# Attention, four experts and a gated layer on one core: seven half-size products parted at token 640 instead of 768

## The chip, the cores and the metric

The program runs on one core of one Trainium2 chip. The metric is the device time of one execution in microseconds (us), lower is better. An execution is profiled besides; its trace gives every instruction's start and duration. PE is the matrix engine, PEld its weight loads, DVE the vector engine, ACT the scalar engine, POOL the GpSimd engine, SP the engine that issues the transfers.

## The reference, cut to what matters

```python
scores = q @ k.T / 8; keep the 32 largest of each row of 576; softmax; x = attn @ v   # 2 x 8 heads, head size 64
x = x.reshape(1152, 512)                                                           # tokens x model
p = probs / probs.sum(-1)
x = sum(p[:, e:e+1] * (relu(x @ w1[e]) @ w2[e]) for e in range(4))                 # hidden size 1024
out = ((x @ w_a) * (x @ w_b)) @ w_out                                              # hidden size 1536
```

## The kernel before

The 1152 tokens are nine tiles of 128, in four groups of 1, 2, 3 and 3 tiles (`GROUPS`): columns 0 to 127, 128 to 383, 384 to 767 and 768 to 1151 of the transposed activations `xs`, which are kept as a high and a low part (`xs[:, 0]`, `xs[:, 1]`). A product of two such operands is three matmuls: high by high, high by low, low by high. Attention of a group feeds the experts of that group (`experts`), whose result `y` is turned on PE (`tr`) and written back to `xs` (`replace`, for groups 2 and 3 `combine`). Then comes the gated layer (`gated`), for 6 blocks of two units of w_a, w_b (`d_unit`).

The pair of products x w_a and x w_b of a unit is made by seven products of half the size (`product`, `multiply`). The tokens are parted in two sets (`sets`), each set in two halves of tokens; the seven products take sums of the halves (S1 to S4, made in `combine`, stored in `xt`) with sums of the weights. One product is 2 x 3 matmuls whose width is one half: 384 columns in set 0 (tokens 0 to 767), 192 in set 1 (tokens 768 to 1151). There are 12 units, so 12 x 42 = 504 matmuls for each set. DVE adds the seven results into a buffer `tp` (line 1315), ACT makes the first copy (line 1324), POOL multiplies the gates (line 1318), ACT and POOL split the product into high and low (lines 1335 and 1336), and `second` multiplies it with w_out; its results are added by DVE (line 1360) and leave by SP. All matmuls have line 487, all turns line 490, since helpers record them.

Set 1's halves lie wholly in the last group; set 0's in groups 0 to 2. `combine` of the last group runs between the first two sets of products of the gated layer (`pending`).

Psum has eight banks of 512 columns. In the last stage six (`pps`) take the half-size products and two (`ns`) the results of `second`. Buffers are named pools (`Slots`); a pool gives its buffers out in a fixed order, and a buffer's next user waits for its last one.

Nothing is ordered by hand: every step is an `Op` with an estimated duration, a key and its waits, and `Plan.best` makes 42 trial orders with `Plan.order`, replays each with `Plan.rerun`, and emits the order with the least mean. Each engine then runs its list in order. A change of one estimated duration can so move instructions anywhere in the program.

Of the kernel before, what the change touches and what calls it, by code (L numbers as in the profile page):

```python
# [13 lines left out]
ALU = mybir.AluOpType  # L14
# [74 lines left out]
SEEN, SEEN_PE = 45, 130  # L89
ISSUE, LAND, GBS, LANES = 500, 2100, 320.0, 8  # L90
# [7 lines left out]
class Plan:  # L98
# [37 lines left out]
    def rerun(self, got, draw):  # L136

        free, end, dma, users = {}, {}, 0.0, {}
        last = 0.0
        for op in got:  # L140
            t = free.get(op.engine, 0.0)
            for w in op.waits:
                t = max(t, end[id(w)] + (SEEN_PE if op.engine == "PE" else SEEN))

            for b in op.tiles:
                u = users.get(id(b))
                if u is None:
                    u = users[id(b)] = [max([self.freed.get(k, 0.0) for k in b.slots.cells(b.slot)] or [0.0])]
                t = max(t, u[0] + (SEEN_PE if op.engine == "PE" else SEEN))
            if op.engine == "SP":  # L150
                free["SP"] = t + ISSUE
                dma = max(dma, t + ISSUE) + op.nbytes / GBS
                e = dma + LAND + draw.uniform(0.0, LATE_DMA)
            else:
                free[op.engine] = t + op.hold
                e = t + op.hold + op.lag + (draw.uniform(0.0, LATE_ENGINE) if op.engine != "PE" else 0.0)
            end[id(op)] = e
            last = max(last, e)
            for b in op.tiles:
                k = (b.slots.name, b.slot)  # L160
                self.freed[k] = max(self.freed.get(k, 0.0), e)
        self.freed.clear()
        return last

    def order(self):
# [57 lines left out]
        def pick(engine):  # L223
# [6 lines left out]
            while ready_:  # L230
                item = heapq.heappop(ready_)
                op = item[2]

                ok = not (op.port and free.get("POOL", 0.0) > now)
                for t in op.tiles:
                    if t.slot is None and (t.slots in stuck or place(t) is None):
                        stuck.add(t.slots)
                        ok = False
                if ok:
                    found = op  # L240
                    break
                skipped.append(item)
                if len(skipped) > 60:
                    break
# [4 lines left out]
        while len(done) < len(self.ops):  # L249
            moved = False  # L250
            for engine in free:
# [15 lines left out]
                if engine == "SP":  # L267
                    free[engine] = now + ISSUE
                    dma_free = max(dma_free, now + ISSUE) + op.nbytes / GBS
                    end = dma_free + LAND  # L270
                    lanes.append(end)
                else:
                    free[engine] = now + op.hold
                    end = now + op.hold + op.lag + op.late
# [41 lines left out]
def mm_r(n):  # L316
    return max(n, 96) / 2.4 + 13.3
# [18 lines left out]
def body(tc, q, k, v, probs, w1, w2, wa, wb, wo, out):  # L336
# [111 lines left out]
    tps = [low.slots("tpa", 1, 4 * 384), low.slots("tpb", 2, 4 * 192)]  # L448
# [182 lines left out]
    def start_pair(c, h2, n):  # L631
# [72 lines left out]
        for b in batches(tiles):  # L704
# [5 lines left out]
            if b not in vrem_done:  # L710
                vrem_done[b] = [
                    load(lambda b=b, j=j: vrem[b][j * REM:(j + 1) * REM, j::2], lambda b=b, j=j: last_rows(v, b)[:, j::2], n - 2.4, (), (), 65536, since=14e3)
# [251 lines left out]
    def second(hts, units, t0, after, bank=None, begin=True, end=True, last=None):  # L964
# [3 lines left out]
        for i, ((h, hd, n), (u, ud, uv, part)) in enumerate(zip(hts, units)):  # L968
# [7 lines left out]
            hd = hd[t0 // 384] if isinstance(hd[0], list) else hd  # L976
# [67 lines left out]
    sets = [(0, 384, 384), (768, 960, 192)]  # L1044
    xdone2, late_x = {}, []

    def combine(c, y, yd):
# [8 lines left out]
        xv = lambda i: xt.ap.rearrange("p (i o a n) -> p i o a n", i=2, o=3, a=2)[:, i, :, :, 384 * own:384 * own + n]  # L1056
        x0, x1 = slice(c0, c0 + n), slice(c1, c1 + n)
        K = -1500 if own else -1000
        got = []

# [9 lines left out]
        def pool(w, emit, key, after, tiles):  # L1070
            if own:
                return vector(dve(w), lambda: emit(nc.vector), key, after, tiles, port=True)
            return gpsimd(pool_(w), lambda: emit(nc.gpsimd), key, after, tiles)

        def half(a):
            tp = tps[own].tile()
            tv = lambda i, j=None: tp.ap[:, i * n:(j or i + 1) * n]
            (p, po), (q_, qo) = turned(a), turned(a + 2)
            if own:
                h1 = scalar(n, lambda: nc.scalar.activation(xs[:, 0, a, x0], p.ap[:, 0:n], AF.Copy), K, [po], [p])  # L1080
                l1 = vector(dve(n), lambda: nc.vector.tensor_tensor(xs[:, 1, a, x0], p.ap[:, 0:n], xs[:, 0, a, x0], op=ALU.subtract), K, [h1], [p])
                got.extend([h1, l1])
                f = [scalar(2 * n, lambda: nc.scalar.activation(tv(0, 2), p.ap[:, 0:2 * n], AF.Copy), K, [po], [p, tp])]
                qv = lambda: q_.ap[:, n:2 * n]
            else:
                f = [
                    pool(n, lambda e, k=k, i=i: e.tensor_tensor(tv(i), xs[:, 0, k, x0], xs[:, 1, k, x0], op=ALU.add), K, ydone[0, k] + ydone[1, k], [tp])
                    for k, i in ((a, 0), (a + 2, 2))
                ]
                f.append(scalar(n, lambda: nc.scalar.activation(tv(1), p.ap[:, 0:n], AF.Copy), K, [po], [p, tp]))  # L1090
                qv = lambda: q_.ap[:, 0:n]
            h = scalar(384, lambda: nc.scalar.activation(xs[:, 0, a + 2, cs], q_.ap[:, 0:384], AF.Copy), K, [qo], [q_])
            l = vector(dve(384), lambda: nc.vector.tensor_tensor(xs[:, 1, a + 2, cs], q_.ap[:, 0:384], xs[:, 0, a + 2, cs], op=ALU.subtract), K, [h], [q_])
            s1 = vector(dve(n), lambda: nc.vector.tensor_tensor(tv(3), qv(), tv(1), op=ALU.add), K, f + [qo], [q_, tp])
            s3 = pool(n, lambda e: e.tensor_tensor(tv(1), tv(1), tv(0), op=ALU.subtract), K, [s1], [tp])
            s2 = pool(n, lambda e: e.tensor_tensor(tv(0), tv(3), tv(0), op=ALU.subtract), K, [s3], [tp])
            if own:
                s4 = vector(dve(n), lambda: nc.vector.tensor_tensor(tv(2), q_.ap[:, 0:n], tv(0), op=ALU.subtract), K, [s2], [q_, tp])
            else:
                s4 = pool(n, lambda e: e.tensor_tensor(tv(2), tv(2), tv(0), op=ALU.subtract), K, [s2], [tp])  # L1100
            h1 = scalar(n, lambda: nc.scalar.activation(xs[:, 0, a, x1], tv(3), AF.Copy), K, [s1], [tp], sbuf=True)
            l1 = pool(n, lambda e: e.tensor_tensor(xs[:, 1, a, x1], tv(3), xs[:, 0, a, x1], op=ALU.subtract), K, [h1], [tp])
            t3 = lambda: tv(0, 3).rearrange("p (o n) -> p o n", o=3)
            h2 = scalar(3 * n, lambda: nc.scalar.activation(xv(0)[:, :, a], t3(), AF.Copy), K, [s4], [tp, xt], sbuf=True)
            l2 = pool(3 * n, lambda e: e.tensor_tensor(xv(1)[:, :, a], t3(), xv(0)[:, :, a], op=ALU.subtract), K, [h2], [tp, xt])
            got.extend([h, l, h1, l1, h2, l2])
        for a in range(2):
            half(a)
        xdone2[own] = got + ([] if own else sum((ydone[g, k] for g in range(2) for k in range(KD)), []))
# [163 lines left out]
    def gated():  # L1273
# [9 lines left out]
        def operand(i, own, hl, a):  # L1283
# [5 lines left out]
            return xt()[:, hl, i - 4, a, 384 * own:384 * own + w]  # L1289
# [16 lines left out]
        def multiply(un, own, g):  # L1306

            m = sets[own][2]
            tp = tps[own].tile()
# [30 lines left out]
        for f in range(F2 // 256):  # L1340
# [80 lines left out]
```

## Time and profile before

| what | value |
|---|---|
| time, median of 3 runs (range) | 847.09 us (846.9 to 849.94) |
| the profiled execution: time, span of its instructions | 847.36 us, 845.6 us |
| mean granted clock of PE | 0.988 |
| busy in the span: PE, PEld, DVE, ACT, POOL | 809.6, 720.0, 771.4, 537.3, 364.8 us |

The time is the whole execution's; the span runs from the first to the last instruction, 1.76 us less. Busy time of PE is from modelled ends, so two matmuls that overlap in the pipe are counted once; how dense they are is read from the distance between their starts.

### The profile page before, as it was taken

What the parts mean: (1) busy time and instruction counts of PE and PEld (TensorE: products, weight loads), DVE (VectorE), ACT (ScalarE), POOL (GpSimd) and SP (SyncE); (2) the same over time, 40 slices, a digit from 0 to 9 for tenths busy, and PEclk for the clock granted to TensorE, in tenths of its full rate; (3) what the DMA queues carried; (4) which work ended last, traced back from release to release, by engine and by line L of the source; (5) the groups of instructions that cost most, each with busy time, mean ns of one, the idle gap of its engine ahead of it and who ended that gap; (6) DMA issues with size and microseconds to landing.
All of it is one profiled execution on the core that took longest, in us unless ns stands there. A gap on an engine that the chain in (4) does not pass through costs nothing.

```text
span 845.6 us, 14637 instructions
## 1 busy us (share of the span) xinstructions
PE 809.6 (96%) x5285; PEld 720.0 (85%) x5285; DVE 771.4 (91%) x1507; ACT 537.3 (64%) x951; POOL 364.8 (43%) x335
## 2 busy tenths in 40 slices
PE   6589999999999999999999999999999999999997
PEld 5467777799888899998999988999889989999895
DVE  7989999999899999999976989998898988989973
ACT  6879887999888989987764656665444423323220
POOL 3524343788979668754210180000024426153431
PEclk9699999999999999999999999999999999999999
DMA  5939976755565343423344646887431312313013
GB/s 175 290 103 335 315 230 206 219 183 179 161 197 178 101 145 118 163 77 100 100 127 145 203 125 221 252 257 259 132 100 52 125 50 76 111 40 100 26 50 112
DMA packets 91416, 129.68 MB, mean 153 GB/s; under 512 B 10832, under 2 KB 67152, under 8 KB 89808
## 3 DMA queue, kind: packets, MB, share of 16 engines
q1 hardware_dynamic: 91344, 128.75, 48.0%
q8 instruction: 41, 0.67, 0.3%
q14 instruction: 31, 0.25, 0.1%
HBM read 115.36 MB, written 13.37 MB: 152 GB/s over the span
## 4 chain that ended last, share of the span: by engine, by line
PE 60%; DVE 22%; ACT 9%; POOL 5%; issue 3%; DMA 1%; POOLq 0%; DVEq 0%; ACTq 0%
PE ps L487 57%; DVE low L767 7%; DVE low L775 6%; PE ps L490 3%; ACT low L806 1%; POOL mid L933 1%; ACT low L817 1%; ACT mid L932 1%; ACT lowa L746 1%; DVE mid L933 1%; DVE big L1269 1%; ACT low L798 1%; DVE raw L1360 1%; ACT lowa L875 1%; POOL low L802 1%
## 5 line engine op out<-in xcount | busy, mean ns | idle before, releaser
L487 PE MATMUL ps<-mid 128*128 128x512 f32 x1092 | 282.2, 397 | 4.0 <-POOL mid L933 2.1
L487 PEld LDWEIGHTS ps<-mid 128*128 128x128 f32 x1092 | 199.3, 189 | 43.5 <-DVE raw L1360 4.0
L487 PE MATMUL ps<-xs,mid 128*128 128x384 f32 (+1 forms) x1152 | 206.1, 321 | 3.3 <-DVE mid L1006 2.6
L487 PEld LDWEIGHTS ps<-xs,mid 128*128 128x128 f32 x1152 | 185.2, 189 | 13.4 <-DVE mid L1006 4.2
L767 DVE MAX8 low<-low 128x8 f32<-128x576 f32 x216 | 154.8, 749 | 0.2
L1318 POOL TENSOR_TENSOR low<-low 128x384 f32<-128x384 f32 (+1 forms) x48 | 48.2, 1005 | 218.9 <-DVE low L1315 217.1
L933 POOL TENSOR_TENSOR mid<-raw,mid 128x1024 fp32r<-128x1024 f32 x48 | 115.0, 2404 | 9.5 <-ACT mid L932 7.3
L802 POOL TENSOR_TENSOR low<-lowa,low 128x576 f32<-128x576 f32 x70 | 101.3, 1462 | 31.1 <-ACT low L798 31.0
L932 ACT ACTIVATE mid<-raw 128x1024 fp32r<-128x1024 f32 x96 | 101.8, 1068 | 16.8 <-PE ps L487 8.5
L775 DVE MATCH_REPLACE8 low<-low 128x576 f32<-128x576 f32 x144 | 106.3, 745 | 0.0
L487 PE MATMUL ps<-xs,big 128*128 128x384 f32 (+1 forms) x576 | 93.3, 307 | 1.8 <-ACT low L1324 1.7
L487 PEld LDWEIGHTS ps<-xs,big 128*128 128x128 f32 x576 | 85.5, 190 | 4.9 <-ACT low L1324 2.0
L1315 DVE TENSOR_TENSOR low<-ps,low 128x384 f32<-128x384 f32 (+1 forms) x168 | 71.8, 449 | 17.0 <-PE ps L487 15.7
L1002 ACT ACTIVATE mid<-ps 128x384 fp32r<-128x384 f32 (+1 forms) x96 | 44.0, 460 | 45.1 <-PE ps L487 40.2
L487 PE MATMUL ps<-lowa_again,big 128*128 128x384 f32 (+1 forms) x432 | 70.8, 305 | 0.0
L933 DVE TENSOR_TENSOR mid<-raw,mid 128x1024 fp32r<-128x1024 f32 x48 | 62.5, 1305 | 5.9 <-ACT mid L932 5.8
L487 PEld LDWEIGHTS ps<-lowa_again,big 128*128 128x128 f32 x432 | 64.4, 190 | 1.4
L1006 DVE SCALAR_TENSOR_TENSOR mid<-ps,mid 128x384 fp32r<-128x384 f32 (+1 forms) x96 | 47.9, 503 | 16.9 <-ACT mid L1002 16.8
L798 ACT ACTIVATE low<-lowa,low 128x576 f32<-128x576 f32 x70 | 53.3, 782 | 12.7 <-POOL low L792 12.6
L817 ACT ACTIVATE low<-low 128x576 f32<-128x576 f32 x70 | 51.9, 782 | 12.3 <-DVE low L814 12.1
L490 PE MATMUL ps<-identr,low 128*128 128x128 f32 x360 | 51.9, 279 | 7.7 <-ACT low L817 7.7
L806 ACT ACTIVATE low<-low 128x576 f32<-128x576 f32 x70 | 54.8, 785 | 4.0 <-POOL low L802 4.0
(121 smaller groups left out, 1235.1 us busy)
## 6 DMA issues: line engine op xcount, KB each, us to landing
raw<-in_moe_w_dram SPq DMA_DIRECT2D x122, 512.0 KB, 3.8
big<-kscr SPq DMA_DIRECT2D x20, 576.0 KB, 5.6
low<-in_v_dram SPq DMA_DIRECT2D x24, 256.0 KB, 3.7
low<-in_moe_w_b_dram SPq DMA_DIRECT2D x12, 512.0 KB, 3.6
low<-in_moe_w_a_dram SPq DMA_DIRECT2D x12, 512.0 KB, 3.6
low<-in_moe_w_out_dram SPq DMA_DIRECT2D x12, 512.0 KB, 4.8
wscr<-big SPq DMA_DIRECT2D x6, 1024.0 KB, 5.5
mid<-wscr SPq DMA_DIRECT2D x6, 1024.0 KB, 4.7
```

Source lines behind the costliest of these rows:

```text
L487: nc.tensor.matmul(out, l, r, **kw)
L490: nc.tensor.transpose(out, a, i)
L767: 62 + 1.04 * width, lambda at=at, cs=cs: nc.vector.max(m8v()[:, x, cs], at()), key + 0.02 * r, [done],
L775: lambda at=at, cs=cs: nc.vector.match_replace(out=src[1](), in_to_replace=m8v()[:, x, cs], in_values=at(), imm_value=LOW),
L798: S, lambda x=x, s=s: nc.scalar.activation(ev(x), s.ap, AF.Relu, bias=endv()[:, x, 1:2], scale=-STEEP),
L802: pool_(S), lambda x=x, s=s: nc.gpsimd.tensor_tensor(ev(x), s.ap, ev(x), op=ALU.subtract), ks, [a], [s, ep]
L806: lambda x=x: nc.scalar.activation(ev(x), ev(x), AF.Exp, bias=endv()[:, x, 0:1], scale=scale, accum_out=sums.ap[:, x:x + 1]),
L817: S, lambda x=x: nc.scalar.activation(ev(x), ev(x), AF.Copy, scale=sums.ap[:, x:x + 1]),
L932: hi = scalar(1024, lambda: nc.scalar.activation(u.ap[:, 0:1024], r.ap, AF.Copy), 500 + s, [ld], [u, r], sbuf=True)
L933: sub = lambda eng: eng.tensor_tensor(u.ap[:, 1024:2048], r.ap, u.ap[:, 0:1024], op=ALU.subtract)
L1315: return vector(dve(m), lambda: nc.vector.tensor_tensor(tv(out), p.ap[:, 0:m], tv(i), op=ALU.add), K, [o] + after, [p, tp])
L1318: return gpsimd(pool_(m), lambda: nc.gpsimd.tensor_tensor(tv(out), tv(i), tv(j), op=ALU.mult), K, after, [tp])
```

## The change

The sets become tokens 0 to 639 in halves of 320, and tokens 640 to 1151 in halves of 256. Set 1 so begins with the last tile of group 2. In `combine`, group 2 is now turned and stored by `replace` as group 1 is, and the sums of set 0 are made by POOL from the stored parts (`whole`, line 1084 of the changed kernel); of set 1, POOL makes the sums of the first 128 tokens and the rest comes from the turned `y`. The buffers `tp` become one pool of two that both sets share, in place of one buffer for set 0 and two for set 1. In the last block, `second` takes two of three results into the six product banks. The planner's estimates change as well: a matmul costs at least 111 ns, PE's steps before 46 us cost 1.7 times as much, a pool is marked as stuck only by the buffer that is next in its order, and one load of v may start at 20 us instead of 14.

```diff
-    return max(n, 96) / 2.4 + 13.3
+    return max(n / 2.4 + 13.3, 111.0)
...
+COLD, COLD_END = 1.7, 46e3
+            hold = op.hold * COLD if op.engine == "PE" and t < COLD_END else op.hold
...
                     if t.slot is None and (t.slots in stuck or place(t) is None):
-                        stuck.add(t.slots)
+                        if t.n == t.slots.next:
+                            stuck.add(t.slots)
                         ok = False
...
-    tps = [low.slots("tpa", 1, 4 * 384), low.slots("tpb", 2, 4 * 192)]
+    tps = low.slots("tp", 2, 4 * 320)
...
-    sets = [(0, 384, 384), (768, 960, 192)]
+    sets = [(0, 320, 320), (640, 896, 256)]
...
+        if not own:
+            replace(c, y, yd)
...
+        def whole(out, k, cols, tp):
+            w = cols.stop - cols.start
+            return gpsimd(
+                pool_(w), lambda: nc.gpsimd.tensor_tensor(out(), xs[:, 0, k, cols], xs[:, 1, k, cols], op=ALU.add), K,
+                sum((ydone[g, k] for g in range(len(GROUPS) - 1)), []), [tp]
+            )
...
+            if own:
...
+                f = [
+                    scalar(384, lambda: nc.scalar.activation(tp.ap[:, 128:512], p.ap[:, 0:384], AF.Copy), K, [po], [p, tp]),
+                    scalar(128, lambda: nc.scalar.activation(tp.ap[:, 640:768], q_.ap[:, 0:128], AF.Copy), K, [qo], [q_, tp]),
+                    whole(lambda: tp.ap[:, 0:128], a, slice(c0, e), tp), whole(lambda: tp.ap[:, 512:640], a + 2, slice(c0, e), tp),
+                ]
...
+            else:
+                f = [whole(lambda: tv(0), a, x0, tp), whole(lambda: tv(1), a, x1, tp), whole(lambda: tv(2), a + 2, x0, tp), whole(lambda: tv(3), a + 2, x1, tp)]
...
-            tp = tps[own].tile()
+            tp = tps.tile()
...
-                gts.append((g, [gd[0, part], gd[0, part], gd[1, part]], n))
+                gts.append((g, [gd[0, part], gd[1, part]], n))
...
-                p, o = second(gts, [un_o + (0,), un_o + (1,)], t * 128, (), ns.tile())
+                p, o = second(gts, [un_o + (0,), un_o + (1,)], t * 128, (), (pps if 2 * f + 2 >= F2 // 128 and t % 3 else ns).tile())
```

PE where the gated layer begins, before. `identr,low` are the turns of the last group's `y`, `xs,big` and `lowa_again,big` the half-size products, `mid` 128x512 the matmuls of `second`:

```order
571 L490 MATMUL ps<-identr,low 128x128 x3
572 L487 MATMUL ps<-xs,big 128x384 x6
573 L490 MATMUL ps<-identr,low 128x128 x9
574 L487 MATMUL ps<-xs,big 128x384 x6
575 L487 MATMUL ps<-lowa_again,big 128x384 x12
576 L487 MATMUL ps<-xs,big 128x384 x12
577 L487 MATMUL ps<-lowa_again,big 128x384 x6
578 L487 MATMUL ps<-xs,big 128x384 x6
579 L487 MATMUL ps<-xs,big 128x192 x6
```

The same place of the changed kernel, where `L491` and `L494` are the old lines 487 and 490:

```order
547 L494 MATMUL ps<-identr,low 128x128 x12
548 L491 MATMUL ps<-xs,big 128x320 x6
549 L491 MATMUL ps<-lowa_again,big 128x320 x12
550 L491 MATMUL ps<-xs,big 128x320 x12
551 L491 MATMUL ps<-lowa_again,big 128x320 x6
552 L491 MATMUL ps<-xs,big 128x320 x6
553 L491 MATMUL ps<-mid 128x512 x6
554 L491 MATMUL ps<-xs,big 128x256 x6
```

The twelve turns now stand together behind all products of the first set, and six matmuls of `second` stand ahead of set 1's first product.

POOL at the same place, before (line 1105 ends the sums of set 0, lines 1318 and 1336 are the gates of the first products):

```order
208 L1105 TENSOR_TENSOR lowa_again<-low,lowa_again 128x3x384
209 L1318 TENSOR_TENSOR low<-low 128x384 x2
210 L1336 TENSOR_TENSOR mid<-low,mid 128x768
211 L1318 TENSOR_TENSOR low<-low 128x384 x2
212 L1336 TENSOR_TENSOR mid<-low,mid 128x768
```

POOL there in the changed kernel, where lines 1115, 1329 and 1347 are the old 1105, 1318 and 1336:

```order
207 L1115 TENSOR_TENSOR lowa_again<-low,lowa_again 128x3x320
208 L1329 TENSOR_TENSOR low<-low 128x320 x2
209 L1084 TENSOR_TENSOR low<-xs 128x128 x2
210 L1347 TENSOR_TENSOR mid<-low,mid 128x640
211 L1084 TENSOR_TENSOR low<-xs 128x128 x2
212 L1329 TENSOR_TENSOR low<-low 128x320 x2
```

Set 1's sums now pass POOL: two for its first half of features behind the first gates, two for the second half behind the split of the first gates, whose `tp` buffer they take over.

ACT in the third step of attention, before (line 806 is the exponential, line 903 the store of an attention result that waits for PE, lines 746 and 552 copy scores and q):

```order
51 L746 ACTIVATE lowa<-ps 128x576
52 L806 ACTIVATE low<-low 128x576
53 L903 ACTIVATE xf<-ps 128x128
54 L552 ACTIVATE big<-low 128x2x2x64
55 L806 ACTIVATE low<-low 128x576
56 L746 ACTIVATE lowa<-ps 128x576
```

ACT there in the changed kernel, where lines 750, 810, 556, 837 and 907 are the old 746, 806, 552, 833 and 903:

```order
57 L810 ACTIVATE low<-low 128x576
58 L750 ACTIVATE lowa<-ps 128x576
59 L556 ACTIVATE big<-low 128x2x2x64
60 L810 ACTIVATE low<-low 128x576
61 L556 ACTIVATE big<-low 128x2x2x64
62 L837 ACTIVATE low<-lowa,low 128x576
63 L907 ACTIVATE xf<-ps 128x128
```

The store of the attention result has moved from ahead of the second exponential to behind it.

## Rows read from the trace of the kernel before

**Rows 1.** The page: busy time of the engines, and the chain that ended last.
```profile
PE 809.6 (96%) x5285; PEld 720.0 (85%) x5285; DVE 771.4 (91%) x1507; ACT 537.3 (64%) x951; POOL 364.8 (43%) x335
PE 60%; DVE 22%; ACT 9%; POOL 5%; issue 3%; DMA 1%; POOLq 0%; DVEq 0%; ACTq 0%
```

**Rows 2.** Busy time of each engine by stage: stretch, length, then engines with instructions.
```profile
0.00:60.00 60.00, 41.70 (x278) 35.05 (x279) 53.01 (x117) 44.25 (x91) 22.53 (x42) 0.86 0.60 184
...
140.00:510.00 370.00, 363.53 (x2586) 326.07 (x2585) 346.13 (x679) 294.28 (x526) 223.91 (x179) 1.00 0.48 149
510.00:612.80 102.80, 102.33 (x515) 92.44 (x514) 93.57 (x151) 58.50 (x88) 0.00 (x0) 1.00 0.70 226
612.80:644.60 31.80, 30.10 (x199) 28.62 (x198) 29.16 (x66) 13.47 (x26) 13.19 (x12) 1.00 0.24 75
...
826.70:845.60 18.90, 13.77 (x56) 9.53 (x55) 6.55 (x10) 0.53 (x1) 2.27 (x4) 0.98 0.36 125
```

**Rows 3.** PE in order of time inside the gated layer: start, us, instructions.
```profile
707.25 2.25 PE L487 MATMUL ps<-xs,big 128*128 128x384 f32 x12
709.33 1.20 PE L487 MATMUL ps<-lowa_again,big 128*128 128x384 f32 x6
...
712.06 1.50 PE L487 MATMUL ps<-lowa_again,big 128*128 128x192 f32 x12
713.40 1.50 PE L487 MATMUL ps<-xs,big 128*128 128x192 f32 x12
```

**Rows 4.** PE in order of time in the experts of group 1.
```profile
171.25 0.52 PE L487 MATMUL ps<-xs,mid 128*128 128x256 f32 x3
171.61 0.86 PE L487 MATMUL ps<-mid 128*128 128x512 f32 x3
```

**Rows 5.** PE in order of time, and of the last chain one step of DVE.
```profile
716.08 2.93 PE L487 MATMUL ps<-mid 128*128 128x512 f32 x12
718.85 1.23 PE L487 MATMUL ps<-xs,big 128*128 128x384 f32 x6
...
826.75 14.11 PE L487 MATMUL ps<-mid 128*128 128x512 f32 x54
...
829.03 0.70 DVE raw L1360
```

**Rows 6.** All engines in order of time where the last group joins the gated layer.
```profile
625.37 1.94 POOL L1336 TENSOR_TENSOR mid<-low,mid 128x768 fp32r<-128x768 f32 x1 [1.12 <-ACT mid L1335]
...
627.34 0.49 ACT L1324 ACTIVATE low<-ps 128x384 f32<-128x384 f32 x1 [0.41 <-POOL mid L1336]
...
627.88 2.70 PE L487 MATMUL ps<-xs,big 128*128 128x384 f32 x12 [1.66 <-ACT low L1324]
```

**Rows 7.** ACT and DVE in order of time in the third step of attention.
```profile
46.57 0.28 ACT L903 ACTIVATE xf<-ps 128x128 f32<-128x128 f32 x1 [0.80 <-PE ps L487]
...
48.42 0.17 DVE L814 RECIPROCAL low<-low 128x2 f32<-128x2 f32 x1 [1.93 <-POOL low L811]
```

**Rows 8.** PE's waits from 140 to 510 us, and one of them in order of time.
```profile
PE ps L487 <- POOL mid L933: 2.6, 2, 2.1
...
288.04 4.38 PE L487 MATMUL ps<-mid 128*128 128x512 f32 x11 [2.11 <-POOL mid L933]
```

**Rows 9.** All engines in order of time around one end of set 0.
```profile
810.74 1.50 PE L487 MATMUL ps<-lowa_again,big 128*128 128x192 f32 x12
...
812.96 1.91 POOL L1336 TENSOR_TENSOR mid<-low,mid 128x768 fp32r<-128x768 f32 x1 [0.96 <-ACT mid L1335]
```

**Rows 10.** Busy time of each engine in four blocks of the gated layer.
```profile
644.63:681.00 36.37, 36.27 (x219) 33.20 (x218) 34.64 (x65) 18.65 (x31) 13.71 (x11) 1.00 0.29 95
681.00:716.08 35.08, 35.08 (x217) 32.73 (x215) 30.46 (x62) 9.65 (x16) 13.77 (x12) 1.00 0.24 76
716.08:752.00 35.92, 35.92 (x219) 33.63 (x218) 33.96 (x64) 11.52 (x18) 12.98 (x13) 1.00 0.23 73
752.00:788.00 36.00, 36.00 (x219) 33.71 (x219) 33.12 (x63) 10.29 (x17) 13.18 (x12) 1.00 0.28 88
```

More of the change, by code (lines that the diff above doesn't have):

```diff
@@ L154, in rerun @@
             else:
-                free[op.engine] = t + op.hold
-                e = t + op.hold + op.lag + (draw.uniform(0.0, LATE_ENGINE) if op.engine != "PE" else 0.0)
+                free[op.engine] = t + hold
+                e = t + hold + op.lag + (draw.uniform(0.0, LATE_ENGINE) if op.engine != "PE" else 0.0)
             end[id(op)] = e
@@ L272, in order @@
                 else:
-                    free[engine] = now + op.hold
-                    end = now + op.hold + op.lag + op.late
+                    hold = op.hold * COLD if engine == "PE" and now < COLD_END else op.hold
+                    free[engine] = now + hold
+                    end = now + hold + op.lag + op.late
                 heapq.heappush(queue, (end, op.n, op))
@@ L711, in start_pair @@
                 vrem_done[b] = [
-                    load(lambda b=b, j=j: vrem[b][j * REM:(j + 1) * REM, j::2], lambda b=b, j=j: last_rows(v, b)[:, j::2], n - 2.4, (), (), 65536, since=14e3)
+                    load(lambda b=b, j=j: vrem[b][j * REM:(j + 1) * REM, j::2], lambda b=b, j=j: last_rows(v, b)[:, j::2], n - 2.4, (), (), 65536, since=20e3)
                     for j in range(2)
@@ L1055, in combine @@
         xt = late_x[0]
[L1056 removed]
+        xv = lambda i: xt.ap.rearrange("p (i o a n) -> p i o a n", i=2, o=3, a=2)[:, i, :, :, 320 * own:320 * own + n]
         x0, x1 = slice(c0, c0 + n), slice(c1, c1 + n)
@@ L1068, in turned, with pair_ @@
             return p, tensor(T * TURN_F, emit, 1000 + nxt(), list(yd.values()), [p, y])
-        def pool(w, emit, key, after, tiles):
+        def pair_(w, emit, after, tiles, sbuf=True):
             if own:
-                return vector(dve(w), lambda: emit(nc.vector), key, after, tiles, port=True)
-            return gpsimd(pool_(w), lambda: emit(nc.gpsimd), key, after, tiles)
+                return vector(dve(w), lambda: emit(nc.vector), K, after, tiles, port=sbuf)
+            return gpsimd(pool_(w), lambda: emit(nc.gpsimd), K, after, tiles)
@@ L1096, in half @@
[L1096 to L1100, printed above, removed]
+                (p, po), (q_, qo) = turned(a), turned(a + 2)
+                e = cs.start
+                h1 = scalar(128, lambda: nc.scalar.activation(xs[:, 0, a, e:e + 128], p.ap[:, 0:128], AF.Copy), K, [po], [p])
@@ L1107, in combine @@
+            got.extend([h1, l1, h2, l2])
         for a in range(2):
             half(a)
-        xdone2[own] = got + ([] if own else sum((ydone[g, k] for g in range(2) for k in range(KD)), []))
+        xdone2[own] = got + sum((ydone[g, k] for g in range(len(GROUPS) - 1) for k in range(KD)), [])
     def replace(c, y, yd):
@@ L1288, in operand @@
                 return xs[:, hl, a + 2 * (i == 2), c1:c1 + w]
-            return xt()[:, hl, i - 4, a, 384 * own:384 * own + w]
+            return xt()[:, hl, i - 4, a, 320 * own:320 * own + w]
         A11, A12, A22, S1, S2, S3, S4 = range(7)
@@ L1308, in multiply @@
             m = sets[own][2]
-            tp = tps[own].tile()
+            tp = tps.tile()
             tv = lambda i, j=None: tp.ap[:, i * m:(j or i + 1) * m]
```

32 lines of the change are left out of this document (12 added, 20 removed).

## The prediction

> **What bounds the kernel now.** I read the page first, to see which engine has no time to spare: PE is busy for 96% of the span and carries 60% of the chain that ended last; DVE is busy for 91% [rows 1]. An average hides stages, so the table by stage comes next [rows 2]. To 60 us PE is busy for 41.7 us and DVE for 53.0: attention's search for the 32 largest scores, on DVE, sets the pace. From 140 us on PE has next to no idle time: 6.5 us in 370 us of experts and attention, 0.5 us in the next 103 us, 1.7 us where the last group joins the gated layer, and in the gated layer almost none [rows 2, 10]. There a matmul that takes less time moves the end, as long as DVE keeps up: in the first block after the join DVE is busy for 34.6 of 36.4 us [rows 10]. The last 19 us are the results of `second` and the transfers out [rows 2].
>
> A busy PE can still be slow, so for prices I divide the distance between starts by the count. Twelve matmuls of 384 columns start 707.25 to 709.33: 173.3 ns each. Twelve of 192 start 712.06 to 713.40: 111.7 ns [rows 3]. Half the columns cost 64%, not 50%. Three of 256 take 171.25 to 171.61: 120 ns [rows 4]. Twelve of 512 take 716.08 to 718.85: 230.8 ns [rows 5]. From 192 to 256 the price rises by 8 ns, from 256 to 384 by 53: below some 230 columns it is nearly flat, above it grows with the columns. A half of 192 columns lies on the flat part.
>
> **The change part by part.**
>
> *The split: -9.2 us.* Each set has 504 matmuls, now 173.3 + 111.7 = 285.0 ns a pair. After it, 256 columns cost 120 ns and 320, which no row shows, 146.7, the mean of 120 and 173.3: 266.7 ns. 504 x 18.3 ns = 9.2 us. Bounds: with the slope from 384 to 512 (57.5 ns for 128 columns) 320 columns cost 144.6, and 10.3 us are saved; on the straight line from 192 to 384 they cost 152.8, and 6.1 us are saved. I take the middle, since 320 lies between two measured widths on the growing part. Columns in all, and the work of DVE, ACT and POOL per unit, stay: 384 + 192 = 320 + 256.
>
> A rule speaks against this. The Trainium skill, page "TensorE: Matmul & The Clock Gate", section "Back-to-back issue gap", gives a lone matmul columns / 2.4 + 2.5 ns; by it both splits cost 245 ns a pair and the saving is nil. The same section says that the weight load counts in a stream too and that the formula is then too low for few columns, and section "LDWEIGHTS" gives 106.7 ns for 128 columns of weights; the rows' 111.7 ns agrees with that, not with the 82.5 ns of the lone formula.
>
> *Two more of three results in the product banks at the end: -1.5 us.* The last 54 matmuls take 14.11 us; 54 x 230.8 ns, and 0.16 us for the last one's own length (2.93 less 2.77 in the row of twelve), are 12.6. The difference is PE waiting for the 0.70 us sum that frees a result bank [rows 5]. With eight banks DVE still needs only 0.70 us of each 1.38 us tile. Bounds: 0, if the product banks come free late, to 1.5; I take 1.5, since the last sums of products end before the second tile needs its bank. The last set's gates are hidden: set 0's split ends 4.1 us after its products (810.74 to 814.87, [rows 9]), set 1 has fewer columns, and five tiles of set 0 (6.9 us) stand ahead of the first tile that needs it.
>
> *The join of the last group: 0.* Before, PE waits 1.66 us for ACT's first copy, which waits until POOL's split frees the one `tp` buffer of set 0 at 627.31 [rows 6]. That goes, but its place is taken: the second half's sums need the first set's buffer. By the order POOL now does two small sums, the split, two more small sums. Counted from the last product of the first set: the split ends after about 3.4 us (4.1 x 320/384) plus two small sums, at most 0.5 us each by POOL's 1.91 us for 768 columns [rows 9]; then two more, and a sum on DVE: some 5.5 us until the turned tiles leave their banks. PE has only three free product banks until then: twelve turns (at most 111.7 ns each) and 18 matmuls are 4.0 us, so it waits about 1.5 us. Set 1's sums end some 3.5 us later, covered by 24 more matmuls (3.5 us) and the six matmuls of `second` (1.4 us). I take 0, with bounds -1.7 and +3.
>
> *DVE with less room: +1.5 us.* 84 pairs a block save 1.5 us of PE; DVE's 34.64, 30.46, 33.96 and 33.12 us then stand in 34.8, 33.5, 34.4 and 34.5 us. Where DVE fills 95% already, in the first block, it has not been shown to do more. If 95.2% is its limit, the first, third and fourth block last 36.4, 35.7 and 34.8 us, and 3.1 us of the gain are lost; if it can be full, 0. I take half.
>
> *The order of attention's third step: -0.8 us.* ACT's store of the attention result idles 0.80 us for PE ahead of the second exponential, and DVE waits 1.93 us for the sum behind that exponential [rows 7]. The store now stands behind it. About 1.2 us of DVE's wait go, and DVE sets the pace there; part is lost when PE takes over. Bounds: -1.9 (the wait gone) and +1.9 (another as long).
>
> *Everything from 140 to 510 us: 0.* The new estimates reorder PE, DVE and ACT here. PE's idle time is 6.5 us, the largest wait 2.1 us for POOL; the 11 matmuls behind it took 4.38 us where 230.8 ns each are 2.54 [rows 2, 8]. So at most 8.3 us are to be had, and the columns and instructions are the same. A new order can have other waits of the same sort: 0, bounds -5 and +5. POOL's extra sums of set 0 (eight of 320 columns instead of four of 384) lie there and in the 103 us after it, in which POOL does nothing [rows 2].
>
> Sum: 847.36 - 9.2 - 1.5 - 0.8 + 1.5 = 837.4 us, against the profiled execution, whose span of 845.6 us has 1.76 us around it. The median of the runs is 0.27 us lower: **837 us**.
>
> **The rivals.**
>
> *DVE becomes the bound of the gated layer.* For it: rows 10, the first block. Against it: the second block needs 87%, and PE's six banks let DVE lag. Then most of the 9.2 us go: 840.5 to 846, say 843.
>
> *The new order of the experts is better.* For it: the 8.3 us of losses, and a pool that no longer holds back an instruction whose buffer is next in turn. Against it: 42 orders were tried before too. With 6 us more: 831.
>
> *The split saves nothing*, since the price grows evenly with the columns, of which there are as many as before. Then 320 and 256 lie on the line from 192 to 384, 152.8 + 132.2 = 285.0 ns, and the time is 837 + 9.2 - 1.5 = 845 (DVE loses nothing then). Rows 4's 120 ns speak against it. This is what the lone formula of the Trainium skill above would give.
>
> *Slower: two `tp` buffers for both sets.* Set 1 had two of its own. Now each set's first copy waits for the split of the set before the last one. If the split came later than the set between, each of 22 sets would wait. A set of 256 lasts 42 x 120 ns = 5.0 us, the split ends 3 to 3.4 us after its products, so 1.6 us are left, and six products into free banks give 36 x 120 ns = 4.3 us more. To end 4.2 us above before, it must eat the 10 us saved too: 14.2 / 22 = 0.65 us a set, so POOL or DVE would have to lag 1.6 + 4.3 + 0.65 = 6.6 us in every set. From there on it decides.
>
> *Slower by the order:* the reordered experts would need 14 us of new waits where the whole stretch now has 6.5.
>
> **How the numbers follow.** The likeliest case (837, own range 833 to 840.5) gets 0.64; DVE as bound 0.14; a better order 0.12; no saving from the split 0.04; the shared buffers 0.03; a worse order 0.03. About 0.5% (4.2 us) is what a measurement tells from no change. Faster, below 842.9: 0.64 + 0.12 + two thirds of the DVE case = 0.86. Same: the rest of the DVE case and the split without saving, 0.09. Slower: 0.05. The range 831 to 843 leaves out a third of the better orders, a third of the DVE case and the last three: about 0.18.
>
> **What would show it.** In the changed profile, starts of 320-column products 147 ns apart and of 256-column ones 120; busy PE in the gated layer with DVE's waits for PE shorter than now; the last 54 matmuls in 12.6 us; one wait of 1 to 2 us at the join; DVE's wait at about 47 us shorter. Wrong, if the 320s are 153 ns apart, if PE shows waits on DVE's sums in the blocks, or if the stretch to the join is longer or shorter than before by over 5 us.

## The result and the profile after

The changed kernel takes 840.94 us (median of 4 runs, 840.02 to 842.72), the kernel before 847.61 us beside it: a ratio of 0.9919, with a 95% interval of 0.9893 to 0.9946. Run again on another occasion it took 840.13 us, 0.9915 [0.9901, 0.9929]. It is faster by 6.7 to 7.4 us; 10 us had been forecast. The execution profiled below is the slowest of the four, 842.72 us with a span of 840.9.

The page: busy time of the engines and the chain that ended last, to hold against [rows 1].

```profile
PE 804.1 (96%) x5285; PEld 715.3 (85%) x5285; DVE 779.1 (93%) x1507; ACT 537.6 (64%) x953; POOL 370.2 (44%) x345
PE 54%; DVE 27%; ACT 6%; POOL 5%; issue 5%; DMA 2%; SPq 0%; DVEq 0%; POOLq 0%; ACTq 0%
```

DVE has as many instructions as before and is busy for 7.7 us more; its share of the chain rose from 22 to 27%. That is where to look. By stage (the columns are those of [rows 2]; the last stretch begins behind the last product):

```profile
0.00:60.00 60.00, 44.83 (x286) 37.66 (x287) 54.40 (x122) 44.53 (x92) 22.68 (x42) 0.94 0.60 188
...
140.00:510.00 370.00, 361.80 (x2572) 325.89 (x2571) 346.29 (x678) 294.66 (x526) 226.16 (x184) 0.99 0.47 148
...
615.70:644.10 28.40, 25.59 (x187) 24.83 (x186) 27.04 (x58) 13.12 (x26) 12.13 (x12) 1.00 0.21 75
644.10:812.60 168.50, 166.12 (x1023) 150.87 (x1023) 160.34 (x298) 55.27 (x89) 66.32 (x56) 1.00 0.23 76
...
823.70:840.90 17.20, 12.51 (x57) 10.04 (x55) 6.60 (x10) 0.63 (x1) 2.77 (x3) 0.93 0.39 137
```

In the blocks, where PE had next to no idle time before [rows 10], 2.4 of 168.5 us are idle now, and 2.8 of 28.4 us at the join. From 140 to 510 us PE is idle for 8.2 us instead of 6.5 [rows 2]. Two stretches there also ran at the lower of PE's two clock levels, 1.2 instead of 2.4 GHz, each behind a wait of PE:

```profile
162.70:166.10 3.40, 3.40 (x13) 3.11 (x14) 3.40 (x9) 3.35 (x6) 1.97 (x2) 0.50 0.60 178
282.10:285.60 3.50, 3.50 (x18) 3.50 (x17) 3.50 (x8) 3.50 (x5) 3.50 (x3) 0.51 0.70 202
```

In attention's third step, DVE's reciprocal, which waited 1.93 us [rows 7], waits for nothing:

```profile
46.85 0.15 DVE L818 RECIPROCAL low<-low 128x2 f32<-128x2 f32 x1
```

The prices, from the distances between the starts of PE's matmuls:

```profile
616.60 1.92 PE L491 MATMUL ps<-lowa_again,big 128*128 128x320 f32 x12
618.36 0.90 PE L491 MATMUL ps<-xs,big 128*128 128x320 f32 x5
...
819.46 1.60 PE L491 MATMUL ps<-lowa_again,big 128*128 128x256 f32 x12
820.90 1.60 PE L491 MATMUL ps<-xs,big 128*128 128x256 f32 x12
...
823.78 12.43 PE L491 MATMUL ps<-mid 128*128 128x512 f32 x54
```

Twelve of 320 columns start 1.76 us apart, 146.7 ns each; twelve of 256 start 1.44 us apart, 120 ns each. The last 54 take 12.43 us instead of 14.11 [rows 5].

Where the last group joins, all engines in order of time:

```profile
625.08 0.41 DVE L1104 TENSOR_TENSOR low<-ps,low 128x256 f32<-128x256 f32 x1
625.28 1.57 POOL L1347 TENSOR_TENSOR mid<-low,mid 128x640 fp32r<-128x640 f32 x1 [0.23 <-ACT mid L1346]
625.60 1.53 DVE L1108 TENSOR_TENSOR low<-low 128x256 f32<-128x256 f32 x1
626.93 1.13 POOL L1084 TENSOR_TENSOR low<-xs 128x128 f32<-128x128 f32 x2
...
629.53 0.41 DVE L1108 TENSOR_TENSOR low<-low 128x256 f32<-128x256 f32 x1
629.87 0.95 DVE L1115 TENSOR_TENSOR lowa_again<-low,lowa_again 128x768 fp32r<-128x768 f32 x1
630.91 0.44 ACT L1335 ACTIVATE low<-ps 128x320 f32<-128x320 f32 x1 [1.05 <-DVE lowa_again L1115]
...
631.40 1.15 PE L491 MATMUL ps<-xs,big 128*128 128x320 f32 x6 [2.76 <-ACT low L1335]
```

PE waits 2.76 us for ACT's first copy, which waits for the `tp` buffer that DVE's step of line 1115 frees. One DVE step, line 1108, takes 1.53 us beside POOL's split and 0.41 us without it. This pattern returns inside the blocks:

```profile
704.63 1.62 POOL L1329 TENSOR_TENSOR low<-low 128x256 f32<-128x256 f32 x2 [0.96 <-DVE low L1326]
...
704.80 0.85 DVE L1229 TENSOR_SCALAR low<-low 128x512 uint32<-128x512 uint32 x1
...
705.68 1.11 DVE L1232 TENSOR_TENSOR low<-low 128x512 f32<-128x512 f32 x1
...
706.99 1.29 POOL L1347 TENSOR_TENSOR mid<-low,mid 128x512 fp32r<-128x512 f32 x1 [0.74 <-ACT mid L1346]
707.12 1.72 DVE L1237 TENSOR_TENSOR low<-low 128x512 f32<-128x512 f32 x1
708.76 1.87 DVE L1326 TENSOR_TENSOR low<-ps,low 128x320 f32<-128x320 f32 x4
...
709.29 1.16 PE L491 MATMUL ps<-lowa_again,big 128*128 128x320 f32 x6 [0.89 <-DVE low L1326]
```

Lines 1229, 1232 and 1237 unpack weights of a later unit, from buffer to buffer. Beside POOL they take 0.85, 1.11 and 1.72 us; in the mean of the run without POOL's gates 0.42, 0.68 and 0.68 (below). The sums that empty PE's banks (line 1326) are queued behind them, and PE waits 0.89 us. These are PE's waits from 600 us on; the kernel before has the join's 1.7 us and 0.2 us besides:

```profile
PE ps L491 <- ACT low L1335: 2.8, 1, 2.8
PE ps L491 <- DVE low L1326: 1.5, 3, 0.9
PE ps L491 <- DVE raw L1371: 0.6, 2, 0.4
```

The distances between starts, added up over all products (504 of each width), sum the gated layer in one number: 92.2 us for 384 columns and 56.1 for 192 before, together **148.3**; 80.8 for 320 and 62.9 for 256 after, together **143.7**. By the medians of the distances (174 and 111 ns before, 147 and 120 after) a pair costs 18 ns less, 9.1 us in all. So 9.1 us came, and 4.5 were lost in the same stage: 1.1 at the join, the other 3.4 in the blocks. The experiments ask where.

### The profile page after: what moved, and what is told of

It reads as the page before. It is cut to its first block, busy times and chain, and to the rows that moved or that the text cites. A ratio compares the mean times of both kernels' runs of the same rounds, so it can differ in the third digit from the quotient of the medians.

```text
span 840.9 us, 14655 instructions
## 1 busy us (share of the span) xinstructions
PE 804.1 (96%) x5285; PEld 715.3 (85%) x5285; DVE 779.1 (93%) x1507; ACT 537.6 (64%) x953; POOL 370.2 (44%) x345
## 4 chain that ended last, share of the span: by engine, by line
PE 54%; DVE 27%; ACT 6%; POOL 5%; issue 5%; DMA 2%; SPq 0%; DVEq 0%; POOLq 0%; ACTq 0%
PE ps L491 50%; DVE low L771 7%; DVE low L779 5%; PE ps L494 4%; DVE low L1326 4%; DVE low L1227 1%; POOL mid L937 1%; DVE low L1035 1%; DVE mid L1010 1%; ACT low L802 1%; POOL low L1084 1%; ACT lowa L750 1%; DVE low L1237 1%; DVE low L1232 1%; DVE mid L937 1%
## 5 line engine op out<-in xcount | busy, mean ns | idle before, releaser
L491 PE MATMUL ps<-mid 128*128 128x512 f32 x1092 | 277.3, 395 | 4.2 <-ACT mid L1006 1.8
L491 PEld LDWEIGHTS ps<-mid 128*128 128x128 f32 x1092 | 199.0, 188 | 42.1 <-DVE mid L1010 3.0
L491 PE MATMUL ps<-xs,mid 128*128 128x384 f32 (+1 forms) x1152 | 204.5, 323 | 2.7 <-DVE mid L1010 2.4
L491 PEld LDWEIGHTS ps<-xs,mid 128*128 128x128 f32 x1152 | 186.2, 191 | 11.0 <-DVE mid L1010 3.3
L1329 POOL TENSOR_TENSOR low<-low 128x320 f32<-128x320 f32 (+1 forms) x48 | 48.5, 1011 | 210.3 <-DVE low L1326 208.7
L806 POOL TENSOR_TENSOR low<-lowa,low 128x576 f32<-128x576 f32 x70 | 98.9, 1430 | 35.4 <-ACT low L802 35.3
L491 PE MATMUL ps<-xs,big 128*128 128x320 f32 (+1 forms) x576 | 88.6, 299 | 3.6 <-ACT low L1335 2.8
L491 PEld LDWEIGHTS ps<-xs,big 128*128 128x128 f32 x576 | 80.7, 189 | 7.6 <-ACT low L1335 3.0
L1326 DVE TENSOR_TENSOR low<-ps,low 128x320 f32<-128x320 f32 (+1 forms) x168 | 71.2, 451 | 10.2 <-PE ps L491 8.4
L491 PE MATMUL ps<-lowa_again,big 128*128 128x320 f32 (+1 forms) x432 | 66.8, 298 | 1.0 <-DVE low L1326 0.9
L491 PEld LDWEIGHTS ps<-lowa_again,big 128*128 128x128 f32 x432 | 60.7, 190 | 3.6 <-DVE low L1326 2.3
L821 ACT ACTIVATE low<-low 128x576 f32<-128x576 f32 x70 | 51.5, 783 | 16.3 <-DVE low L818 16.2
L494 PE MATMUL ps<-identr,low 128*128 128x128 f32 x360 | 52.8, 283 | 8.8 <-ACT low L821 7.8
L494 PEld LDWEIGHTS ps<-identr,low 128*128 128x128 f32 x360 | 42.7, 144 | 18.2 <-ACT low L821 11.6
```

The source lines that it names most:

```text
L491: nc.tensor.matmul(out, l, r, **kw)
L494: nc.tensor.transpose(out, a, i)
L806: pool_(S), lambda x=x, s=s: nc.gpsimd.tensor_tensor(ev(x), s.ap, ev(x), op=ALU.subtract), ks, [a], [s, ep]
L821: S, lambda x=x: nc.scalar.activation(ev(x), ev(x), AF.Copy, scale=sums.ap[:, x:x + 1]),
L1326: return vector(dve(m), lambda: nc.vector.tensor_tensor(tv(out), p.ap[:, 0:m], tv(i), op=ALU.add), K, [o] + after, [p, tp])
L1329: return gpsimd(pool_(m), lambda: nc.gpsimd.tensor_tensor(tv(out), tv(i), tv(j), op=ALU.mult), K, after, [tp])
```

## The experiments

Differences are against the changed kernel's 840.13 us and its ratio of 0.9915 unless another kernel is named.

**The changed kernel again, and its parts one by one.**

> The changed kernel once more, beside the three that follow. 840 to 842 us, as measured; its stages give the spread of one order: the first gated product at 615 to 616 us if the 2.5 us lost ahead of it are this order's own, at 612 to 613 if they were chance.

840.13 us. It reaches the first product at 612.2 us instead of 615.7 in the first profile, with the same order, so the late arrival was chance. Some 2 of the 3.5 us are the clock's, an estimate from the starts of the same matmuls ahead of the two places named above and behind them: it stays at 1.00 at both here. Another 1 us is a wait for DVE ahead of the first place, 1.70 us there and 0.67 here. Nine matmuls of 256 columns took 2.25 us in the first profile, at 162.61 us, and take 1.34 here, at 161.02. A wait did not always bring the lower clock: PE waited 1.91 us ahead of the second place in the first profile, and 1.92 us here.

Here it falls to 0.50 behind the join's wait of 2.76 us instead, where the first profile has 1.00:

```profile
628.30:631.70 3.40, 3.40 (x11) 2.93 (x10) 3.40 (x8) 2.10 (x3) 0.00 (x0) 0.50 0.23 80
```

Six matmuls of 320 columns and six of 512 there last 3.94 us up to the next start, 2.38 in the first profile. So single executions can differ by 1 to 2 us at such a place, whatever the change is worth. The products take 143.9 us.

*The two result banks alone,* in the kernel before:

```diff
-second(..., ns.tile())
+second(..., (pps if 2 * f + 2 >= F2 // 128 and t % 3 else ns).tile())
```

> The kernel before with the two added result banks in the last block alone; the order of every engine is that of before. If the wait for result banks is the whole loss of the last 54 matmuls: 12.4 to 12.6 us for them instead of 14.1, and the time 1.5 to 1.7 us lower, 846 us. If DVE's sums or the transfers out set the end instead: no change of the time, with the last transfer as far behind the last sum as now or farther.

844.70 us, 0.9968 [0.9956, 0.9979]: 1.8 to 3.7 us faster. The trace shows 1.7 of them, as expected:

```profile
824.91 12.45 PE L487 MATMUL ps<-mid 128*128 128x512 f32 x54
```

*The planner's edits alone,* with the sets of before parted at 768 and no added banks:

```diff
+COLD, COLD_END = 1.7, 46e3
...
-                        stuck.add(t.slots)
+                        if t.n == t.slots.next:
+                            stuck.add(t.slots)
...
-    return max(n, 96) / 2.4 + 13.3
+    return max(n / 2.4 + 13.3, 111.0)
```

(and the load of v from 20 us on).

> The kernel before with the planner's edits alone, split at 768. Theory 1 (the reordering up to the gated layer costs): 846.5 to 850 us, with the first gated product 1 to 3 us later than before although attention's start is about 1 us ahead. Theory 2 (the reordering gains about 1 us, and the gated layer alone lost what is missing): 845.5 to 846.5 us.

851.09 us, 1.0050 [1.0032, 1.0068]: 3.5 us slower than before, outside the ranges of both theories. The time is not lost ahead of the gated layer, which it reaches at 611.6 us, but in it: the same matmuls take 93.2 + 59.7 = 152.9 us instead of 148.3. These waits of PE in it are new or longer (total us, times, longest us):

```profile
PE ps L491 <- DVE raw L1364: 0.9, 2, 0.7
PE ps L491 <- ACT raw L1361: 0.8, 2, 0.6
PE ps L491 <- DVE low L1319: 0.8, 4, 0.2
```

So a new order alone can lose as much in this stage, 4.6 us, as the changed kernel lost beside the split. That it is the same loss isn't shown: the two orders differ, and these waits add up to 2.5 us only. Against this kernel the split brings 152.9 - 143.7 = 9.2 us of PE.

*The split without most of the rest:* the changed kernel without the added banks, `COLD`, the price of 111 ns and the later load. The edit on stuck pools stays.

> The changed kernel without the two added banks and without three of the planner's edits: matmuls cost columns / 2.4 + 13.3 ns again, PE's first 46 us are not stretched, the load of v may start at 14 us. The mark of a stuck pool stays as changed, since the plan stands still without it. Theory 1 (the split is worth about 6 us net wherever the order falls, DVE and the join taking 3 of 9): 841.5 to 843.5 us with the 14.1 us end of before. Theory 2 (the planner's better price is needed, so that the order fits the matmuls): over 844 us.

844.08 us, 0.9953 [0.9935, 0.9970], and 143.7 us of products: the same loss. The runs spread from 841.6 to 845.8 us, across the ranges of both theories, and don't decide between them. What is left of the planner's edits here is the one on stuck pools; whether it makes the loss, or any order with these sets would, this doesn't tell.

**Is it DVE's amount of work?** First less of it, in both kernels: 8 of 12 units get the low part of their weights for 8 columns only.

```diff
-u.ap[:, (7 + i) * 256:(7 + i + n) * 256], v(i + 1, n), u.ap[:, i * 256:(i + n) * 256]
+u.ap[:, (7 + i) * 256:(7 + i) * 256 + (n * 256 if f < FRONT + 2 else 8)], v(i + 1, n)[:, 0:(n * 256 if f < FRONT + 2 else 8)], u.ap[:, i * 256:i * 256 + (n * 256 if f < FRONT + 2 else 8)]
```

> The changed kernel, with 8 of the 12 units of the gated layer given only the first 8 columns of the low part of their weights, so most of DVE's subtraction there is left out (some 1.85 us of DVE less a unit, 15 us of its 160 in the stage); PE's order is that of the changed kernel. Theory: DVE, busy for 160 of 168.5 us from the last group's join to the last product, now holds PE back by some 3 us of what the split saves there. Then the time falls by 3 to 4 us against the changed kernel's 840.1, and the stretch from the join to the last product from 168.5 to 165 us. Rival: DVE keeps up, and the smaller saving comes from elsewhere (waits at the join, a later arrival). Then the time stays within 1 us of 840.

838.49 us, 0.9903 [0.9887, 0.9919]: about 1 us, inside the intervals. The subtractions (line 1280) take 15 us less, DVE as a whole is busy for 12 us less (767.0 instead of 779.0), and PE still waits for single sums:

```profile
PE ps L491 <- DVE low L1326: 2.0, 2, 1.1
PE ps L491 <- DVE raw L1371: 0.6, 2, 0.4
```

> The same cut of DVE's work (the low part of the weights left out but for 8 columns, in 8 of 12 units) in the kernel before. Theory that only the changed kernel lacks room on DVE: 847.6 falls by at most 1 us. Rival that both lose to DVE alike, or that less work on DVE helps PE by itself: it falls by as much as the changed kernel does, 3 us or more.

845.66 us, 0.9992 [0.9980, 1.0004]: no change that can be told, as expected of the kernel before. But the changed kernel did not give back the 3 to 4 us that the theory of DVE's little room expected of it: that theory has failed. Then more work, the second low part written twice:

```diff
-lambda i=i, n=n: nc.vector.tensor_tensor(...)
+lambda i=i, n=n: [nc.vector.tensor_tensor(...) for _ in range(1 if f < FRONT or i == 0 else 2)]
```

> The changed kernel, with the second of the two subtractions for the low part of a unit's weights made twice in 10 of 12 units: 1.1 us more of DVE for each, 11 us in all. Theory that DVE bounds the gated layer: at 160.3 of 168.5 us only some 5 us are left even if it never waited, so the time rises by 6 to 11 us. Rival that PE's six banks let DVE catch up and it has room: at most 3 us.

856.90 us, 1.0107 [1.0091, 1.0123]: 16 us more, beyond the 6 to 11 expected. The added steps were longer than the 11 us reckoned with: the subtractions take 15.5 us more, and DVE is busy for 14.6 us more (793.6). So more work costs about what DVE needs for it, and less returns next to nothing. PE's waits in the blocks:

```profile
PE ps L491 <- DVE low L1326: 7.4, 11, 1.8
PE ps L491 <- DVE raw L1371: 3.0, 4, 1.8
```

**Is it POOL?** First only at the join:

```diff
+            w = 8 if not own and un is units[0] else 2 * m
+            c8 = slice(cs.start, cs.start + w)
...
-                g.ap[:, n:2 * n][:, cs], tv(0, 2), g.ap[:, 0:n][:, cs]
+                g.ap[:, n:2 * n][:, c8], tv(0, 2)[:, 0:w], g.ap[:, 0:n][:, c8]
```

> The changed kernel, with POOL's low part of the first set's first gates made for only 8 columns (the rest of that low part is left out): 1.6 us less of POOL just where the last group joins; every order is as in the changed kernel. Theory: the turned tiles wait for their buffer because POOL's low part runs beside DVE's sum of the first half (1.53 us instead of 0.41) and ahead of POOL's second pair of sums. Then PE's wait there falls from 2.8 to about 1.2 us or less and the time by 1 to 2 us. Rival: the wait is set by the order of DVE's own steps, and stays between 2.3 and 2.8 us.

838.84 us, 0.9904 [0.9891, 0.9916]: in the time it can't be told from the changed kernel. PE waits 1.67 us instead of 2.76, more than the 1.2 expected, and line 1108 takes 0.71 us instead of 1.53. POOL's step is the cause of 1.1 us of the wait. In the rest ACT's copy still waits for DVE's step of line 1115, at the end of a row of DVE's sums.

Then all of POOL's gates:

```diff
-nc.gpsimd.tensor_tensor(tv(out), tv(i), tv(j), op=ALU.mult)
+nc.gpsimd.tensor_tensor(tv(out)[:, 0:8], tv(i)[:, 0:8], tv(j)[:, 0:8], op=ALU.mult)
...
-g.ap[:, n:2 * n][:, cs], tv(0, 2), g.ap[:, 0:n][:, cs]
+g.ap[:, n:2 * n][:, c8], tv(0, 2)[:, 0:8], g.ap[:, 0:n][:, c8]
```

> The changed kernel, with POOL's gate products and its low part of the gates made for only 8 columns in all 12 units of both sets (the other columns of the gates are left as unmultiplied sums, those of their low part unwritten): some 80 us less of POOL in the gated layer; every order is that of the changed kernel. In the traces so far DVE's steps that read and write only buffers take up to 1.7 us instead of 0.4 to 0.7 beside such a step of POOL; summed over the gated layer DVE is lengthened by some 13 us in the kernel before and 20 us in the changed one. Theory: these long single steps are what PE waits for in the blocks, and what the split loses. Then the lengthening falls to 3 us or less, PE's time above the prices of its matmuls from the first to the last product falls from 10 to 5 us, and the time by 4 to 6 us against the changed kernel's 840. Rival: DVE's own amount of work or its order makes PE wait; then at most 2 us, as much as the join's shorter wait.

831.38 us, 0.9818 [0.9805, 0.9830]: 8.2 us faster, more than expected. The products take 75.9 + 60.6 = 136.5 us, 7.2 less, and PE's only wait from 600 us on is the join's 1.7. Cutting the gates takes POOL's own time away too, but that was not what PE waited for: from 600 us on, no wait of PE or DVE in the changed kernel ends with a step of POOL, and PE waits for ACT, which does wait for POOL, at the join alone. DVE's steps in the gated layer (busy us, mean ns of one), in the changed kernel:

```profile
L1326 DVE TENSOR_TENSOR low<-ps,low 128x320 f32<-128x320 f32 x84 | 38.8, 485 | 5.0 <-PE ps L491 4.5
...
L1237 DVE TENSOR_TENSOR low<-low 128x512 f32<-128x512 f32 x17 | 14.2, 836 | 0.1
...
L1232 DVE TENSOR_TENSOR low<-low 128x512 f32<-128x512 f32 x17 | 13.3, 783 | 0.2
...
L1229 DVE TENSOR_SCALAR low<-low 128x512 uint32<-128x512 uint32 x17 | 9.6, 567 | 0.2
```

and without POOL's gates:

```profile
L1326 DVE TENSOR_TENSOR low<-ps,low 128x320 f32<-128x320 f32 x82 | 38.2, 485 | 8.3 <-PE ps L491 7.4
...
L1232 DVE TENSOR_TENSOR low<-low 128x512 f32<-128x512 f32 x17 | 11.7, 685 | 0.2
...
L1237 DVE TENSOR_TENSOR low<-low 128x512 f32<-128x512 f32 x17 | 11.6, 681 | 0.1
L1229 DVE TENSOR_SCALAR low<-low 128x512 uint32<-128x512 uint32 x17 | 7.1, 419 | 0.2
```

The sums that take an operand from a bank keep their 485 ns. Steps from buffer to buffer shrink from 836 to 681, 783 to 685 and 567 to 419 ns. All such steps for the weights together (the busy time of their groups by their count): 107.7 us for 148, a mean of 728 ns, in the changed kernel; 88.6 us for 145, 611 ns, without the gates. The Trainium skill, "SBUF — State Buffer", section "Who interferes with whom", names both kinds: a DVE instruction with two inputs in buffers waits where GpSimd reads buffers, so does `tensor_scalar` in a mode that takes both ports, and one with a single such input does not. The rows agree in all three; that line 1229's `tensor_scalar` ran in such a mode no row shows.

> The same cut of POOL's work (gate products and the low part of the gates for only 8 columns) in the kernel before. Theory that only the changed kernel, with less room on DVE, loses PE time to DVE's long steps beside POOL: 847 falls by 1 to 3 us, most of it the wait at the join (1.7 us, which hangs on POOL's low part) and 0.5 us of small waits. Rival that the steps cost both kernels alike: it falls by as much as the changed kernel does.

844.82 us, 0.9974 [0.9964, 0.9984]: 1.8 us, of which 0.6 at the join. The kernel before has the same lengthening to a lesser degree, 104.1 us for 153 steps, 680 ns, against 92.7 us for 152, 610 ns, without POOL's gates, and loses little PE time to it. The planner's edits at the old split (the kernel of 851.09 us) have 719 ns, 107.2 us for 149. Counted from the first product to the last, 40 of 157 such steps start under a step of POOL in the kernel before, 47 of 151 in that one and 49 of 147 in the changed kernel. So a new order of the steps puts more of DVE's unpacking beside POOL even with the old widths. That kernel was not run without POOL's gates, so its 4.6 us are not shown to come from this. With POOL's gates cut in both, the products take 146.7 and 136.5 us: without the collisions the split is worth 10.2 us.

**Two whole kernels that try to take something back.**

```diff
+            if not own and un is units[0]:
+                return [hi, vector(dve(2 * m), lambda: nc.vector.tensor_tensor(
+                    g.ap[:, n:2 * n][:, cs], tv(0, 2), g.ap[:, 0:n][:, cs], op=ALU.subtract), K, [hi], [g, tp], port=True)]
```

> A whole computation: the changed kernel, with DVE instead of POOL making the low part of the first set's first gates, one step ahead of the first half's first sum; all else in the same order. Theory that POOL's step, by lengthening that sum and by holding the buffer, sets the wait at the join: DVE needs 0.8 us for it, the sum takes 0.41 instead of 1.53 and POOL's second pair of sums comes sooner; PE's wait falls from 2.8 to some 1.7 to 2.1 us and the time by about 1 us against the changed kernel. Rival: DVE's 0.8 us more in its row eats it, and the wait stays between 2.5 and 3 us.

839.25 us, 0.9917 [0.9902, 0.9932]: not to be told from the changed kernel. The wait at the join is 2.2 us instead of 2.76, just above the theory's 1.7 to 2.1, and 0.6 us is too little to be seen in the time.

```diff
-            got += [hi, vector(dve(n * 256), ...tensor_tensor(...))]
+            got += [hi, gpsimd(pool_(n * 256), ...) if i == 0 and f >= FRONT else vector(dve(n * 256), ...)]
```

> A whole computation: the changed kernel, with POOL instead of DVE making the first, 768 columns wide low part of the weights in 10 of 12 units, planned anew: DVE loses 10 steps of 1.0 to 1.4 us, POOL gains 10 of some 1.9 us. Theory that DVE's steps are held while POOL runs: what DVE saves it loses to longer other steps, and the time stays within 2 us of the changed kernel's 840 or rises. Rival that DVE's amount of work is the limit: 2 to 4 us faster.

841.07 us, 0.9931 [0.9918, 0.9944]: DVE has 10 steps less, the time is no shorter. PE's waits for DVE from 600 us on:

```profile
PE ps L491 <- DVE low L1327: 2.0, 4, 0.8
PE ps L491 <- DVE raw L1372: 0.8, 3, 0.3
```

The Trainium skill, "Perfetto Trace Analysis", section "Optimizing Scalar/DVE Operations", warns that handing DVE's work to GpSimd might not help, since the two share a port. Here it did not.

None of the kernels that compute everything beats the changed one measurably. A kernel with the new sets and banks in an order that keeps DVE's unpacking clear of POOL was not tried; the kernel without the gates gives an estimate of what it could bring, 8 us.

## Why the prediction was right, and by how much it missed

The direction and the range held: 840.9 lies within 831 to 843. The point was 3.9 us too low, and the likeliest case's own range, 833 to 840.5, was missed by 0.4 us in the first measurement and held in the second (840.13). One sign that the forecast had named for being wrong did appear: PE waits on DVE's sums in the blocks, 1.5 us in three waits. The terms:

| term | forecast, us | measured, us |
|---|---|---|
| the split | -9.2 | -9.1 by medians, -9.2 against the planner's edits alone |
| two more of three result banks | -1.5 | -1.7 in the traces; -1.8 to -3.7 in the times |
| the join | 0 | +1.1 |
| DVE with less room | +1.5 | +3.4 lost in the blocks, by another cause |
| attention, and 140 to 510 us | -0.8 | 0 to -1.0, not settled |
| sum | -10.0 | -6.3 to -7.3; the times gave -6.7 to -7.4 |

**The split** was priced rightly: 146.7 ns for 320 columns, as taken, and 120 for 256. That the price lies between its two neighbours was reasoned; that it was met to 0.1 ns is luck, since the 120 came from three matmuls. The rival that the split saves nothing is refuted: 285 ns a pair before, 267 after.

**The banks:** 12.43 us for the last 54 against the 12.6 forecast.

**The join** was sized too low, and its mechanism was wrong. The forecast had PE stop after three products, for want of banks. It ran 36 matmuls, six products, into all six banks, and stopped until ACT's copy, which needed the `tp` buffer, emptied the first. That the second half's sums must wait for the first gates' split was in the forecast; that the split would hold up DVE's sum beside it (1.53 us instead of 0.41) was not. Cutting that split took 1.1 us from the wait.

**DVE with less room** is the step that failed. The split's part said that the work of DVE per unit stays, and this one took half of 3.1 us from DVE's share of busy time. The instructions stay; their durations don't. DVE's buffer-to-buffer steps went from 680 to 728 ns in the mean, single ones beside POOL to 1.7 us, and a step that is 1 us longer ahead of a bank's sum can make PE wait whatever the average share: 0.89 us in the row above. DVE does fill 160.3 of 168.5 us in the blocks now, 95.2%, the very share that the forecast had taken as a possible limit, but less work did not move the end: with 12 us less of DVE's busy time the kernel was 1 us faster, without POOL's gates, which took 15 us off DVE's busy time, 8.2.

**The order** is the second failure. It was priced for attention and for 140 to 510 us alone. The wait in attention went as was said, and DVE ends its 200th search step 1.2 us earlier by the medians (156.9 against 158.1 us). What is left of it at the gated layer isn't settled: the first product of the changed order comes at 612.2 to 615.7 us (median 612.8 of seven executions), that of the four in the order of before at 610.9 to 613.1 (median 612.4) with six matmuls of 512 columns (1.4 us) still to do. That is 1.0 us by the medians. But three of the four, and three of the seven, have PE at the lower clock somewhere from 140 to 510 us; of those that have not, the one of before comes at 610.9, the four changed ones at 612.2 to 613.0, so with the 1.4 us next to nothing is gained. The forecast's largest loss in that stretch was such a case: the 11 matmuls of 4.38 us [rows 8] ran at a mean granted clock of 0.61, behind the wait of 2.11 us, so 1.8 of its 8.3 us were the clock's. At the old split the planner's edits cost 3.5 us where the forecast had no term for them, in the gated layer; at the new one no run shows their cost, and the kernel without most of them was no faster.

Of the rivals, DVE as the bound (843) came nearest in size, not in its cause; the two shared `tp` buffers cost nothing beyond the join, the one place where PE waits for ACT's first copy. Open stays which of the planner's edits moves DVE's steps beside POOL's.

## What to carry to other kernels

A saving on the busiest engine is worth its price list only if the engines that feed it keep their durations: read those per operation, beside and away from the other user of their port, not as a share of busy time. When a change alters a planner's estimates, run the estimates alone: at the old split they cost 3.5 us. An engine at 95% can hold others back by single long steps; taking 12 us off it then returned 1, taking the collisions away returned 8. Where two executions of one kernel differ, look at the clock stretch by stretch before explaining it by the order.

## What the runs showed of the hardware

- A DVE step from buffer to buffer that starts under a POOL step took up to 1.72 us instead of 0.68, and 1.53 instead of 0.41; sums with an operand in a bank were not lengthened (485 ns with and without).
- The cost was not symmetric: 14.6 us more of DVE's busy time made the kernel 16 us slower, 12 us less made it 1 us faster.
- Of two profiled executions of the same kernel one came to the gated layer 3.5 us later than the other. It had PE at a granted clock of 0.50 and 0.51 in two stretches, behind waits of 1.70 and 0.32 us and of 1.91 us; the other was at 1.00 in both, behind waits of 0.67 and 0.31 us and of 1.92 us.
